# One transformer-like block on one core: another opening for the first four tiles, and the last output tile in column halves

## The chip, the core and the metric

The kernel runs on one core of one Trainium2 chip. A core has five engines that each work through their own list of instructions in order: TensorE (PE in the profile; its weight loads are listed apart as PEld), VectorE (DVE), ScalarE (ACT), GpSimd (POOL) and SyncE (SP), which here only starts transfers. Transfers between the chip's main memory and the core's working memory run on 16 DMA engines. PE writes its results into a small accumulator memory (PSUM), from which ACT or DVE copies them out; a function on ACT needs the right table, which a table load brings in.

The metric is the device time of one execution in microseconds (us), lower is better. Before the change its median over five runs is 233.13 us (232.92 to 233.24).

## The reference

The input is `A_x`, 2048 rows of 512. Every row is normalized to mean 0 and variance 1 (with 1e-5 added to the variance). From the normalized rows `xn` come two branches, and the result puts them together:

```python
xn = _layernorm(x, axis=-1)
s = _A_ref(xn, A_wqkv, A_wo)
g = _silu(_B_ref(xn, B_w_gate, B_w_up, B_w_down))
return x + s * g
```

Branch A is attention with 32 heads of 16: `q`, `k` and `v` are one product with `wqkv` (512 x 1536); each position attends to 8 earlier positions, 2 apart; the heads' outputs go through `wo` (512 x 512). Branch B is a gated network: `gelu(xn @ w_gate) * (xn @ w_up)`, 1792 wide, then `w_down` back to 512. All data are bf16.

## The kernel before

The 2048 rows are 16 tiles of 128 rows. Four tiles make a quarter `j` (`TQ` = 512 rows, `NJ` = 4). A quarter passes through three stages: `qkv` (12 groups of 4 matmuls, one group for each 128 columns of `wqkv`; groups 0 to 3 are q, 4 to 7 k, 8 to 11 v), `glu` (14 steps `fc`, each with a gate group, an up group, their copies on ACT and a product on DVE) and `down` (one step for each of the four tiles: 14 matmuls for y, Silu on ACT, 4 matmuls for s, a product and a sum on DVE, and the store). The attention's own steps (products `pk` and `pv` on DVE, short matmuls on PE) are hung between these by a table of side steps, `at(...)`. The order is written out by hand: `tc.manual_schedule()` keeps the instructions of each engine in the order of the program, and only the waits between engines are added.

Matmuls contract over 128 at a time, so `project` (L219) runs four matmuls over the contraction blocks `dk` into one PSUM tile. Their right operand is `xnT`, the normalized rows transposed. For a tile of rows the way there is:

- `moments` (L169): `bn_stats` and `bn_aggr` on DVE give mean and variance `mv`; DVE adds EPS; POOL raises the sum to the power -0.5, which gives `rstd`.
- `normalize` (L179): one DVE instruction makes `xn`.
- `transpose` (L186): four PE transposes into one PSUM tile `tr`, then one ACT copy into `xnT`. (Quarters 2 and 3 are transposed by DMA.)

PSUM tiles with the tag `mm` share 5 buffers that are taken in turn: `tr`, the q, k and v groups, the gate and up groups, y and s, and the tile that the warm-up writes.

The opening (L452 to L473) is the part of the program that the change rewrites. PE starts with `warm_up(9, TQ)`: nine matmuls of 512 columns on zeros whose result nobody reads. Then come moments of tiles 0 and 1, their normalization and transposes, with two small warm-up matmuls of 128 columns (`warm_up(2, P)`) behind each set of transposes; then moments and normalization of tiles 2 and 3; then moments of tiles 4 to 7 and constants on POOL. The q and k groups of quarter 0 run in two halves of 256 rows: with `hh` = 0 they need tiles 0 and 1 only, and the transposes of tiles 2 and 3 are put in front of groups 3 and 5. The v groups follow with 512 rows at a time.

All loads are started by SP in the order of L93 to L101: x tiles 0 to 3 one by one, then the q, the k and the v third of `wqkv`, then x tiles 4 to 7, and then the gate and up weights with the rest of x.

The end is `down` for tile 15 (L368). There y is one PSUM tile of 512 columns and Silu one ACT instruction of 512, while s, the product, the sum and the store are done in two pieces of 256 columns. The first piece's store is started by SP, the second's by ACT.

Of the kernel before, what the change touches and what calls it, by code (L numbers as in the profile page):

```python
# [9 lines left out]
AF = mybir.ActivationFunctionType  # L10
# [18 lines left out]
def kernel(  # L29
# [81 lines left out]
            )  # L111


    warm = const.tile([P, TQ], BF16, name="warm")
    nc.vector.memset(warm[:], 0.0)
    ident = const.tile([P, P], BF16, name="ident")
    make_identity(nc, ident[:])
# [48 lines left out]
    rstd = const.tile([P, NT, 1], F32, name="rstd")  # L166


    def moments(t):  # L169
        nc.vector.bn_stats(out=stats[:, t, :], in_=x_sb[:, t, :])  # L170
        nc.vector.bn_aggr(out=mv[:, t, :], in_=stats[:, t, :])
        nc.vector.tensor_scalar(  # L172
            out=rstd[:, t, :], in0=mv[:, t, 1:2], scalar1=EPS, scalar2=None, op0=ALU.add
        )
        nc.gpsimd.tensor_tensor(out=rstd[:, t, :], in0=rstd[:, t, :], in1=mhalf[:], op=ALU.pow)  # L175
# [7 lines left out]
            op0=ALU.subtract, op1=ALU.mult,  # L183
        )

    def transpose(t):  # L186
        xn = xns[t]
        tr = mm.tile([P, NC * P], BF16, name="tr", tag="mm")
        for c in range(NC):
            nc.tensor.transpose(tr[:, c * P : (c + 1) * P], xn[:, c * P : (c + 1) * P], ident[:])  # L190
        j, i = divmod(t, TPQ)
        if i == 0:
            xnT[j] = xtp.tile([P, NC, TQ], BF16, name="xnT")
        nc.scalar.activation(  # L194
            out=xnT[j][:, :, i * P : (i + 1) * P],
            in_=tr[:].rearrange("p (c n) -> p c n", c=NC),
            func=AF.Copy,
        )

    def warm_up(n, cols):  # L200

# [14 lines left out]
                transpose=True,  # L216
            )

    def project(ps, w, lo, j, i0=0, n=TQ):  # L219
        for dk in range(NC):  # L220
            nc.tensor.matmul(  # L221
                ps[:],
                lhsT=w[:, dk, lo : lo + P],
                rhs=xnT[j][:, dk, i0 : i0 + n],
                start=(dk == 0),
                stop=(dk == NC - 1),
            )

    st = [dict(pk={}, pv={}) for _ in range(NJ)]

    def qkv(j, fo, i0=0, n=TQ):
        which, c = divmod(fo, NC)
        if fo == 0 and i0 == 0:
            st[j]["q"] = qp.tile([P, NC, TQ], BF16, name="q_sb")
        ps = mm.tile([P, n], F32, name="qkv_ps", tag="mm")
        project(ps, wqkv_sb, fo * P, j, i0, n)
        if which == 0:
            nc.scalar.activation(out=st[j]["q"][:, c, i0 : i0 + n], in_=ps[:], func=AF.Copy)  # L238
        elif which == 1:
            lo = PAD + j * TQ + i0  # L240
            nc.scalar.activation(out=k_sb[:, c, lo : lo + n], in_=ps[:], func=AF.Copy)  # L241
        else:
            vst = sm4.tile([P, TQ], BF16, name="vst")
            nc.scalar.activation(out=vst[:], in_=ps[:], func=AF.Copy)  # L244
            lo = PAD + j * TQ
            nc.sync.dma_start(out=vT[c * P : (c + 1) * P, lo : lo + TQ], in_=vst[:])
# [119 lines left out]
        st[j][fc] = h  # L366

    def down(j, tt):  # L368
        y = mm.tile([P, D], F32, name="y_ps", tag="mm")
        for fc in range(NF):  # L370
            nc.tensor.matmul(  # L371
                y[:],
                lhsT=st[j][fc][:, tt * P : (tt + 1) * P],
                rhs=wd_sb[:, fc, :],
                start=(fc == 0),
                stop=(fc == NF - 1),
            )
        sl = sm2.tile([P, D], BF16, name="sl")
        nc.scalar.activation(out=sl[:], in_=y[:], func=AF.Silu)  # L379
        t = j * TPQ + tt  # L380
        o_t = sm4.tile([P, D], BF16, name="o_t")
        pieces = 2 if t == NT - 1 else 1
        n = D // pieces
        for i in range(pieces):
            cols = slice(i * n, (i + 1) * n)
            s = mm.tile([P, n], F32, name="s_ps", tag="mm")
            for g in range(NC):
                nc.tensor.matmul(  # L388
                    s[:],
                    lhsT=st[j]["oT"][:, g, tt * P : (tt + 1) * P],  # L390
                    rhs=wo_sb[:, g, cols],
                    start=(g == 0),
                    stop=(g == NC - 1),
                )
            m = sm2.tile([P, n], BF16, name="m")
            nc.vector.tensor_tensor(out=m[:], in0=s[:], in1=sl[:, cols], op=ALU.mult)  # L396
            nc.vector.tensor_tensor(out=o_t[:, cols], in0=m[:], in1=x_sb[:, t, cols], op=ALU.add)  # L397
            (nc.scalar if i else nc.sync).dma_start(
                out=out2d[t * P : (t + 1) * P, cols], in_=o_t[:, cols]
            )  # L400


    side = {}
# [46 lines left out]


    HT = TPQ // 2  # L452
    warm_up(9, TQ)
    moments(0)
    moments(1)
    normalize(0)
    transpose(0)
    normalize(1)
    warm_up(2, P)
    transpose(1)  # L460
    warm_up(2, P)
    moments(2)
    moments(3)
    normalize(2)
    normalize(3)
    for t in range(TPQ, 2 * TPQ):
        moments(t)
    sum_constants()
    for hh in range(2):
        for fo in range(2 * NC):  # L470
            qkv(0, fo, hh * HT * P, HT * P)
            if hh == 0 and fo in (2, 4):
                transpose(HT + fo // 2 - 1)  # L473
    for i in range(NC):
        run("qkv", 0, i)
        run("qkv", 0, NC + i)
# [42 lines left out]
```

## Time and profile before

| | |
|---|---|
| median of five runs | 233.13 us (232.92 to 233.24) |
| the profiled execution | 233.13 us |
| its span, first to last instruction | 231.4 us |
| PE busy | 225.4 us (97% of the span) |
| PEld busy | 104.0 us (45%) |
| DVE busy | 146.5 us (63%) |
| ACT busy | 131.8 us (57%), 14 table loads among it |
| POOL busy | 23.6 us (10%) |
| data moved | 23.71 MB |

The span is 1.7 us shorter than the time of the same execution; the profiled execution took as long as the median run. In lines of the timeline the first number is the start in us from the start of the span, the second the duration of the whole group on that line, then engine, line of the program, operation, output and inputs, shape, and the count; square brackets give the idle time of the engine just before and what ended it. The matmuls on a line overlap, so twelve matmuls of 272 ns can take 1.47 us together. In the groups by line, the first number after the bar is the busy time in us, the second the mean duration of one instruction in ns.

### The profile page before, as it was taken

The page shows a single profiled execution, that of the slowest core. Times are in us where ns is not written, and L with a number is a line of the kernel's source. Part 1 is how long each engine was busy: PE and PEld are TensorE (multiplying, and loading weights), DVE is VectorE, ACT ScalarE, POOL GpSimd, SP SyncE. Part 2 cuts the span into 40 slices and gives each one's busy share as a digit, 9 for nine tenths or more (in the row PEclk, how much of TensorE's full clock was granted, in tenths as well). Part 3 has the DMA queues.
Part 4 walks back from the last instruction along what each step waited for, and adds up shares of the span by engine and source line. Part 5 has one row for each costly group of instructions (what it writes and reads, how often), then busy time and mean ns, then how long its engine had stood idle before and what let it go on. Part 6 is the DMA issues. An engine that isn't in the chain of part 4 may idle for free.

```text
span 231.4 us, 3491 instructions
## 1 busy us (share of the span) xinstructions
PE 225.4 (97%) x1313; PEld 104.0 (45%) x1313; DVE 146.5 (63%) x232; ACT 131.8 (57%) x214; POOL 23.6 (10%) x64
## 2 busy tenths in 40 slices
PE   7899999999999999999999999999999999999993
PEld 2775444444444444444444444444444444444441
DVE  4593996997795198981677149941449429864132
ACT  2779879755514865756721595656642396576211
POOL 3258924100000000130000000000000000000000
PEclk9999999999999999999999999999999999999999
DMA  5999499921388211100276711100047800000001
GB/s 143 363 374 371 114 192 203 299 87 48 89 184 193 60 23 28 26 0 0 92 168 142 164 24 31 23 6 0 24 138 162 202 29 0 0 0 4 23 23 45
DMA packets 27057, 23.71 MB, mean 102 GB/s; under 512 B 6688, under 2 KB 27040, under 8 KB 27040
## 3 DMA queue, kind: packets, MB, share of 16 engines
q1 hardware_dynamic: 26896, 23.42, 38.6%
q8 instruction: 10, 0.16, 0.3%
q10 hardware_dynamic: 144, 0.07, 0.1%
q14 instruction: 7, 0.06, 0.1%
HBM read 18.22 MB, written 4.21 MB: 97 GB/s over the span
## 4 chain that ended last, share of the span: by engine, by line
PE 95%; DVE 2%; DMA 1%; ACT 1%; issue 0%
PE g_ps L221 21%; PE u_ps L221 21%; PE y_ps L371 21%; PE qkv_ps L221 18%; PE s_ps L388 6%; PE o_ps L336 3%; PE L_ps L276 3%; PE tr L190 1%; DMA x_sb<-in_A_x_dram 1%; DVE stats L170 1%; PE den_ps L296 0%; PE sp_ps L311 0%; DVE m L396 0%; ACT sl L379 0%; ACT xnT L194 0%; DVE o_t L397 0%
## 5 line engine op out<-in xcount | busy, mean ns | idle before, releaser
L221 PE MATMUL g_ps<-xnT,wg_sb 128*128 128x512 bf16 x224 | 57.6, 379 | 0.0
L221 PE MATMUL u_ps<-xnT,wu_sb 128*128 128x512 bf16 x224 | 57.5, 379 | 0.0
L371 PE MATMUL y_ps<-wd_sb,h 128*128 128x512 bf16 x224 | 51.0, 379 | 0.0
L365 DVE TENSOR_TENSOR h<-ge,u 128x512 bf16<-128x512 bf16 x56 | 23.8, 424 | 34.1 <-ACT u L363 33.9
L266 DVE TENSOR_TENSOR pk<-q_sb,k_sb 128x2048 bf16<-128x2048 bf16 x32 | 37.8, 1220 | 11.6 <-ACT k_sb L241 11.6
L221 PE MATMUL qkv_ps<-xnT,wqkv_sb 128*128 128x512 bf16 (+1 forms) x224 | 43.0, 349 | 0.6 <-ACT xnT L194 0.6
L361 ACT ACTIVATE ge<-g_ps 128x512 bf16<-128x512 f32 x56 | 33.6, 601 | 14.4 <-PE g_ps L221 12.9
L363 ACT ACTIVATE u<-u_ps 128x512 bf16<-128x512 f32 x56 | 33.6, 599 | 13.9 <-PE u_ps L221 13.9
L322 DVE TENSOR_TENSOR pv<-E,v_arr 128x2048 bf16<-128x2048 bf16 x32 | 38.6, 1217 | 0.1
L379 ACT ACTIVATE sl<-y_ps 128x512 bf16<-128x512 f32 x16 | 9.6, 598 | 43.9 <-PE y_ps L371 43.9
L221 PEld LDWEIGHTS <-wu_sb 128*128 128x128 bf16 x224 | 21.9, 98 | 26.6 <-issue 0.3
L371 PEld LDWEIGHTS <-h 128*128 128x128 bf16 x224 | 21.9, 98 | 26.4
L221 PEld LDWEIGHTS <-wg_sb 128*128 128x128 bf16 x224 | 20.8, 98 | 26.6 <-issue 4.2
L221 PEld LDWEIGHTS <-wqkv_sb 128*128 128x128 bf16 x224 | 21.6, 98 | 19.9 <-issue 0.8
L396 DVE TENSOR_TENSOR m<-s_ps,sl 128x512 bf16<-128x512 f32 (+1 forms) x17 | 11.2, 657 | 26.6 <-PE s_ps L388 24.1
L175 POOL TENSOR_TENSOR rstd<-rstd,mhalf 128x1 f32<-128x1 f32 x16 | 10.5, 654 | 78.3 <-DVE rstd L172 78.3
L388 PE MATMUL s_ps<-wo_sb,oT 128*128 128x512 bf16 (+1 forms) x68 | 16.4, 366 | 0.0
L170 DVE BATCH_NORM_STATS2 stats<-x_sb 128x6 f32<-128x512 bf16 x16 | 11.0, 687 | 4.0 <-DMA x_sb<-in_A_x_dram 4.0
L238 ACT ACTIVATE q_sb<-qkv_ps 128x512 bf16<-128x512 f32 (+1 forms) x20 | 10.2, 512 | 5.4 <-PE qkv_ps L221 5.1
L244 ACT ACTIVATE vst<-qkv_ps 128x512 bf16<-128x512 f32 x16 | 9.6, 597 | 5.6 <-PE qkv_ps L221 5.6
L241 ACT ACTIVATE k_sb<-qkv_ps 128x512 bf16<-128x512 f32 (+1 forms) x20 | 10.2, 512 | 3.2 <-PE qkv_ps L221 2.9
L348 DVE TENSOR_TENSOR oT<-o_ps,rb 128x1024 bf16<-128x1024 f32 x8 | 9.7, 1219 | 1.4 <-PE o_ps L336 1.4
(42 smaller groups left out, 110.8 us busy)
## 6 DMA issues: line engine op xcount, KB each, us to landing
v_arr<-vT SPq DMA_DIRECT2D x16, 520.0 KB, 5.1
vT<-vst SPq DMA_DIRECT2D x16, 128.0 KB, 2.6
out_dram<-o_t SPq DMA_DIRECT2D x15, 128.0 KB, 2.5
wg_sb<-in_B_w_gate_dram SPq DMA_DIRECT2D x2, 896.0 KB
wu_sb<-in_B_w_up_dram SPq DMA_DIRECT2D x2, 896.0 KB, 13.8
wd_sb<-in_B_w_down_dram SPq DMA_DIRECT2D x1, 1792.0 KB, 17.1
wqkv_sb<-in_A_wqkv_dram SPq DMA_DIRECT2D x3, 512.0 KB, 5.6
x_sb<-in_A_x_dram SPq DMA_DIRECT2D x3, 512.0 KB, 10.3
```

The costliest lines, as they stand in the source:

```text
L170: nc.vector.bn_stats(out=stats[:, t, :], in_=x_sb[:, t, :])
L175: nc.gpsimd.tensor_tensor(out=rstd[:, t, :], in0=rstd[:, t, :], in1=mhalf[:], op=ALU.pow)
L221: nc.tensor.matmul(ps[:], lhsT=w[:, dk, lo : lo + P], rhs=xnT[j][:, dk, i0 : i0 + n], start=(dk == 0), stop=(dk == NC - 1),)
L238: nc.scalar.activation(out=st[j]["q"][:, c, i0 : i0 + n], in_=ps[:], func=AF.Copy)
L266: nc.vector.tensor_tensor(out=pk[:], in0=st[j]["q"][:], in1=k_sb[:, :, off : off + TQ], op=ALU.mult)
L322: nc.vector.tensor_tensor(out=pv[:], in0=st[j]["E"][:, wh, :].unsqueeze(1).to_broadcast([P, 4, TQ]), in1=st[j]["va"][:, 4 * g : 4 * g + 4, ...
L361: nc.scalar.activation(out=ge[:], in_=g_ps[:], func=AF.Gelu_apprx_tanh)
L363: nc.scalar.activation(out=u[:], in_=u_ps[:], func=AF.Copy)
L365: nc.vector.tensor_tensor(out=h[:], in0=ge[:], in1=u[:], op=ALU.mult)
L371: nc.tensor.matmul(y[:], lhsT=st[j][fc][:, tt * P : (tt + 1) * P], rhs=wd_sb[:, fc, :], start=(fc == 0), stop=(fc == NF - 1),)
L388: nc.tensor.matmul(s[:], lhsT=st[j]["oT"][:, g, tt * P : (tt + 1) * P], rhs=wo_sb[:, g, cols], start=(g == 0), stop=(g == NC - 1),)
L396: nc.vector.tensor_tensor(out=m[:], in0=s[:], in1=sl[:, cols], op=ALU.mult)
```

## The change

There are three parts.

1. *rstd of tiles 0 to 3.* Instead of an addition on DVE and a power on POOL, ACT computes `Sqrt(variance + EPS)` into `std`, and DVE takes its reciprocal. The reciprocal stands at the start of `first_normalize`, so behind both tiles' moments. A Sqrt on a constant at the very start makes ACT load the table for Sqrt first. Tiles 4 to 15 keep the power on POOL.
2. *The opening.* The warm-up is 17 matmuls of 256 columns on a tile of zeros half as wide, and four instead of two small ones behind each set of transposes. The ACT copy of tile 1's transposes is cut in two parts of two contraction blocks each. The first four q groups are no longer done one after another: all four run over contraction blocks 0 and 1, and then all four over blocks 2 and 3. The transposes of tiles 2 and 3 are placed behind the four q groups and behind group 4, and their copies are done by DVE. The moments of tiles 4 to 7 are placed behind the k groups of the first half.
3. *The last tile.* For tile 15, y and Silu are also computed in halves of 256 columns: y, Silu, s, product, sum and store of the left half, then the same of the right half. Both stores are started by SP.

```diff
-    warm = const.tile([P, TQ], BF16, name="warm")
+    warm = const.tile([P, TQ // 2], BF16, name="warm")
...
+    epsc = const.tile([P, 1], F32, name="epsc")
+    nc.gpsimd.memset(epsc[:], EPS)
+    std = const.tile([P, TPQ, 1], F32, name="std")
+
+    nc.scalar.activation(out=std[:, 0, :], in_=epsc[:], func=AF.Sqrt, bias=epsc[:], scale=1.0)
+
+    def first_moments(t):
+        nc.vector.bn_stats(out=stats[:, t, :], in_=x_sb[:, t, :])
+        nc.vector.bn_aggr(out=mv[:, t, :], in_=stats[:, t, :])
+        nc.scalar.activation(
+            out=std[:, t, :], in_=mv[:, t, 1:2], func=AF.Sqrt, bias=epsc[:], scale=1.0
+        )
+
+    def first_normalize(t):
+        nc.vector.reciprocal(out=rstd[:, t, :], in_=std[:, t, :])
+        normalize(t)
...
-    def transpose(t):
+    def transpose(t, parts=1, copy=None):
...
-        nc.scalar.activation(
-            out=xnT[j][:, :, i * P : (i + 1) * P],
-            in_=tr[:].rearrange("p (c n) -> p c n", c=NC),
-            func=AF.Copy,
-        )
+        dst = xnT[j][:, :, i * P : (i + 1) * P]
+        src = tr[:].rearrange("p (c n) -> p c n", c=NC)
+        for k in range(parts):
+            c = slice(k * NC // parts, (k + 1) * NC // parts)
+            if copy is None:
+                nc.scalar.activation(out=dst[:, c], in_=src[:, c], func=AF.Copy)
+            else:
+                copy(out=dst[:, c], in_=src[:, c])
...
-    def project(ps, w, lo, j, i0=0, n=TQ):
-        for dk in range(NC):
+    def project(ps, w, lo, j, i0=0, n=TQ, dks=range(NC)):
+        for dk in dks:
...
-    def qkv(j, fo, i0=0, n=TQ):
+    def qkv(j, fo, i0=0, n=TQ, ps=None):
...
-        ps = mm.tile([P, n], F32, name="qkv_ps", tag="mm")
-        project(ps, wqkv_sb, fo * P, j, i0, n)
+        if ps is None:
+            ps = mm.tile([P, n], F32, name="qkv_ps", tag="mm")
+            project(ps, wqkv_sb, fo * P, j, i0, n)
...
     def down(j, tt):
-        y = mm.tile([P, D], F32, name="y_ps", tag="mm")
-        for fc in range(NF):
-            nc.tensor.matmul(
...
-        nc.scalar.activation(out=sl[:], in_=y[:], func=AF.Silu)
-        t = j * TPQ + tt
+        t = j * TPQ + tt
+        halves = [slice(0, D // 2), slice(D // 2, D)] if t == NT - 1 else [slice(0, D)]
+        n = D // len(halves)
...
+        for i, cols in enumerate(halves):
+            y = mm.tile([P, n], F32, name="y_ps", tag="mm")
+            for fc in range(NF):
+                nc.tensor.matmul(
+                    y[:],
+                    lhsT=st[j][fc][:, tt * P : (tt + 1) * P],
+                    rhs=wd_sb[:, fc, cols],
+                    start=(fc == 0),
+                    stop=(fc == NF - 1),
+                )
+            nc.scalar.activation(out=sl[:, cols], in_=y[:], func=AF.Silu)
             s = mm.tile([P, n], F32, name="s_ps", tag="mm")
...
-            (nc.scalar if i else nc.sync).dma_start(
-                out=out2d[t * P : (t + 1) * P, cols], in_=o_t[:, cols]
-            )
+            nc.sync.dma_start(out=out2d[t * P : (t + 1) * P, cols], in_=o_t[:, cols])
...
     HT = TPQ // 2
-    warm_up(9, TQ)
-    moments(0)
-    moments(1)
-    normalize(0)
-    transpose(0)
-    normalize(1)
-    warm_up(2, P)
-    transpose(1)
-    warm_up(2, P)
-    moments(2)
-    moments(3)
-    normalize(2)
-    normalize(3)
+    HQ = HT * P
+    warm_up(17, TQ // 2)
+    first_moments(0)
+    first_moments(1)
+    first_normalize(0)
+    transpose(0)
+    first_normalize(1)
+    warm_up(4, P)
+    transpose(1, parts=2)
+    warm_up(4, P)
+    first_moments(2)
+    first_moments(3)
+    first_normalize(2)
+    first_normalize(3)
+
+    qs = [mm.tile([P, HQ], F32, name="qkv_ps", tag="mm") for _ in range(NC)]
+    for dks in ((0, 1), (2, 3)):
+        for fo in range(NC):
+            project(qs[fo], wqkv_sb, fo * P, 0, 0, HQ, dks)
+    for fo in range(NC):
+        qkv(0, fo, 0, HQ, qs[fo])
+    transpose(HT, copy=nc.vector.tensor_copy)
+    for fo in range(NC, 2 * NC):
+        qkv(0, fo, 0, HQ)
+        if fo == NC:
+            transpose(HT + 1, copy=nc.vector.tensor_copy)
     for t in range(TPQ, 2 * TPQ):
         moments(t)
     sum_constants()
-    for hh in range(2):
-        for fo in range(2 * NC):
-            qkv(0, fo, hh * HT * P, HT * P)
-            if hh == 0 and fo in (2, 4):
-                transpose(HT + fo // 2 - 1)
+    for fo in range(2 * NC):
+        qkv(0, fo, HQ, HQ)
```

## The prediction

> **What bounds the kernel now.** I read the page's chain first, then the waits of PE, then the timeline of the first 10 us and of the last 5. The chain says PE for 95% of the span, and PE's list of waits has three entries, all before 7.5 us:
>
> ```profile
> PE 95%; DVE 2%; DMA 1%; ACT 1%; issue 0%
> ```
>
> ```profile
> PE warm_ps L204 <- DVE k_sb L161: 1.3, 1, 1.3
> PE qkv_ps L221 <- ACT xnT L194: 0.6, 1, 0.6
> PE tr L190 <- DVE xn L181: 0.2, 1, 0.2
> ```
>
> So PE works without a break from its first q matmul at 7.49 us to its last s matmul, and only two stretches can be shortened: what lies before 7.49, and what follows PE's end. The opening, in order of time:
>
> ```profile
> 1.25 4.02 PE L204 MATMUL warm_ps<-warm 128*128 128x512 bf16 x9 [1.25 <-DVE k_sb L161]
> 3.75 0.18 DVE L171 BATCH_NORM_AGGREGATE mv<-stats 128x2 f32<-128x6 f32 x1
> 4.28 0.55 POOL L175 TENSOR_TENSOR rstd<-rstd,mhalf 128x1 f32<-128x1 f32 x1 [2.86 <-DVE rstd L172]
> 5.05 0.41 DVE L181 TENSOR_SCALAR xn<-x_sb,mv,rstd 128x512 bf16<-128x512 bf16 x1
> 5.51 0.61 PE L190 MATMUL tr<-ident,xn 128*128 128x128 bf16 x4 [0.24 <-DVE xn L181]
> 6.16 1.28 ACT L194 ACTIVATE xnT<-tr 128x512 bf16<-128x512 bf16 x2 [4.08 <-PE tr L190]
> 6.37 0.43 PE L190 MATMUL tr<-ident,xn 128*128 128x128 bf16 x4
> 7.24 0.10 PEld L221 LDWEIGHTS <-wqkv_sb 128*128 128x128 bf16 x1 [0.50 <-DMA wqkv_sb<-in_A_wqkv_dram]
> 7.49 1.47 PE L221 MATMUL qkv_ps<-xnT,wqkv_sb 128*128 128x256 bf16 x12 [0.57 <-ACT xnT L194]
> 9.02 1.04 PE L221 MATMUL qkv_ps<-xnT,wqkv_sb 128*128 128x256 bf16 x8
> 9.28 0.59 ACT L194 ACTIVATE xnT<-tr 128x512 bf16<-128x512 bf16 x1
> ```
>
> The second copy into xnT ends at 6.16 + 1.28 = 7.44 and releases the q matmuls at 7.49. But the weights for them were there only at 7.24: the weight load of that time waited for their DMA. So at most 7.49 - 7.24 = 0.25 us can be had here, however early xnT is. The end of the kernel:
>
> ```profile
> 226.50 1.04 PE L388 MATMUL s_ps<-wo_sb,oT 128*128 128x256 bf16 x8
> 226.69 0.60 ACT L379 ACTIVATE sl<-y_ps 128x512 bf16<-128x512 f32 x1 [3.29 <-PE y_ps L371]
> 227.33 0.42 DVE L396 TENSOR_TENSOR m<-s_ps,sl 128x256 bf16<-128x256 f32 x1 [2.43 <-ACT sl L379]
> 228.00 0.42 DVE L396 TENSOR_TENSOR m<-s_ps,sl 128x256 bf16<-128x256 f32 x1
> 228.45 0.29 DVE L397 TENSOR_TENSOR o_t<-m,x_sb 128x256 bf16<-128x256 bf16 x1
> 228.77 0.38 ACTq L398 DMA_DIRECT2D out_dram<-o_t  x1
> ```
>
> PE ends at 227.54. The first m waited for Silu (227.29); the second had to stand behind the first pair on DVE and started at 228.00, 0.46 after the last s.
>
> **rstd.** The first copy waits for xn of tile 0, and that does not wait for POOL: pow ends at 4.28 + 0.55 = 4.83, xn starts at 5.05, because DVE first finishes the moments of tile 1 and its addition (4.98). Without the two additions, stats of tile 1 can start about 0.10 after the aggregate at 3.75, so at 3.85 instead of 4.04, and its aggregate ends at 4.75. The Sqrt on ACT: two ACT copies of 512 and 256 columns take 0.597 and 0.385, so 0.83 ns a column and 0.17 fixed; one column is at least 0.17 and at most 0.385. I take 0.26, so std of tile 0 is ready at 3.98 + 0.26 = 4.24, hidden by the moments of tile 1 (0.4 us of cover). The reciprocal of 128x1 is bounded by the additions of that shape (0.15) and the reciprocal of 128x128 (0.952); the shape decides, 0.15. So reciprocal 4.67 to 4.82, xn of tile 0 4.86 to 5.27 (0.19 earlier), and xn of tile 1, whose pow held it at 5.90, at about 5.37 to 5.78.
>
> The dummy Sqrt and its constant (one POOL memset of 0.10, done near 1.5) lie in ACT's idle time before 6.16; the table load at 0.80 (1.28 us) was there already and changes only its table. The rule that speaks against this part is that of the Trainium skill, "ScalarE: Activation LUTs", section "Table sets: the hidden batching unit": keep functions of one set together, a switch costs about 2.66 us. The same section says that cheap functions such as copy are in every set. By its rule alone, Sqrt and Copy in turn would cost two more switches, an estimate of 5.3 us from that page's figure. The trace has 14 loads, none before a Copy that follows Gelu, Exp or Silu, so I count none.
>
> **Warm-up and transposes.** The memset is half as long (0.27 now; PE starts at 1.14 instead of 1.25). Nine matmuls of 512 take (4.02 - 0.63) / 8 = 0.424 each; 17 of half the size at 0.213 end at 4.77, where now it is 5.07. Transposes of tile 0 start at 5.32; they are still at the slow rate (0.107 each: the four at 5.51 take 0.61, those at 6.37 only 0.43). Four small warm-up matmuls behind them keep PE until 6.17, past xn of tile 1 (5.78), so these and no longer POOL set the second transposes: 6.17 against 6.37. The fast rate came near 6.5, so the last is done at about 6.72 (now 6.80). This part of the earlier xn is lost.
>
> **Split copy and interleaved q.** Part one of the copy, 256 columns, 0.385: 6.76 to 7.14; part two to 7.43. Matmuls on blocks 0 and 1 could start at 7.19, the weights at 7.24 decide. That the waits go by the piece and not by the whole xnT is seen above: the fourth q group (9.02) ran beside the copy of tile 2 (9.28) that stands ahead of it in the program. Eight matmuls at (1.47 - 0.27) / 11 = 0.109 take until 8.11, well past part two; the fourth PSUM buffer, freed by part two, is asked for at 7.89. So the opening gains 0.25 at most, 0.15 if the first weight load (0.10) has to be over; nothing if a wait on part two is put ahead. I take 0.23.
>
> **What is moved behind it.** Copies of tiles 2 and 3 go to DVE: between 0.41 (xn, same shape) and 0.69 (m, same shape, from PSUM), at 9.41 and 10.12, done by 10.81 at the worst; the second-half q groups want them at about 11.15. If that cover were gone, each 0.1 late would cost 0.1. ACT is relieved of 2 x 0.59, and its Sqrts of tiles 2 and 3 (near 7.4 to 7.8) are over before the first q copy at 8.5. In the interleaved order that copy comes 0.4 later than now (8.12), four copies follow at 0.34 each, and PSUM buffers come free at 8.9, 9.2, 9.6 and 9.9, ahead of PE's need at 9.20, 9.64, 9.86 and 10.30. Here 0.3 is the least cover. The k third of wqkv lands near 8.7 (issued 3.13, median 5.6 to landing); wanted at 9.2. Moments of tiles 4 to 7 wait for their x until 11.71 now, so DVE loses nothing by their new place; POOL's queue loses four pows, and sum_constants stays behind the later ones. SP's queue keeps its order up to the end. From 7.49 on PE has no idle time with a releaser, so a q start 0.23 earlier moves everything by 0.23, unless a transfer is late then: the v products start at 43.6, and their last DMA (issued at 29.8, at most 11.3 to landing) is there by 41.1; if that cover of 2.5 were gone, the gain of the opening would be lost there.
>
> **The last tile.** PE does the same sums in 28 + 8 matmuls of 256 columns: 28 x 0.109 = 3.05 against 14 x 0.216 = 3.02, so 0.03 longer. The extra weight loads (98 ns) fit under 109. The right y is now done 0.44 before PE's end, Silu of 256 columns (0.385, as the copies) ends 0.02 after it, so PE's last s releases the second m. Behind PE alone m starts 0.10 after (223.74 against 223.64 one tile earlier): 227.54 + 0.03 + 0.10 = 227.67 against 228.00. Gain 0.33; bounds 0.25 (Silu as late as 0.1 more) and 0.40. The store moves from ACT's queue to SP's, where nothing is ahead of it but the left store, over 1 us before; same size, same landing, 0.
>
> **Sum** against the profiled 233.13 (which is the median): -0.23 - 0.33 = -0.56, so 232.57 us.
>
> **Rivals.** (1) *The opening gives nothing* (the split copy released late, or weights landing later in other runs): for it, the margin between part one (7.19) and weights (7.24) is only 0.05, and the gain is capped by a DMA; against it, the piecewise waits. Time 233.13 - 0.33 = 232.80: within 0.2%, which is 0.47 us and about what a measurement can tell from no change. The same result if only the opening holds: 232.90.
>
> (2) *The fast rate of PE comes later* and the change is slower. Now PE runs slow from 1.25 to about 6.5, with an idle stretch of some 0.4 between 5.07 and 5.51. The warm-up will end 0.3 earlier and the gap be 0.55. If the rate counted anew from 5.32 and took the same 5.2 us, q work would run at half rate from 7.24 to 10.5 and lose 1.6: 234.2. It decides the sign from a rate change at 7.24 + 2 x 0.56 = 8.4, and makes it slower by 0.2% from 9.3. Against it: between 3.1 and 6.5 PE is busy for 2.75 us now and by my times for 2.87 after, for the eight small matmuls fill up. The Trainium skill, "TensorE: Matmul & The Clock Gate", Part 1, says that a free-running window of about 3.4 us has to be busy; an estimate from that page, one window missed after 6.5, is 1.3 us of loss.
>
> (3) *Copy is not in Sqrt's table*: reloads of 1.28 before the copies and before Sqrt of tiles 2 and 3 put ACT back by some 2.6 at the first q copy, and PE would wait about 1.7 for buffers: 234.3. Only the 14 loads seen speak against it.
>
> **How the numbers follow.** Forecast with both gains at 0.47 or more: 0.50, range 232.35 to 232.66. One gain only, or both with a small stall: 0.32, between 232.66 and 233.6. Slower: 0.18, of which rival 2 0.10, rival 3 0.03, an unseen stall in the new order 0.05. Low end: opening 0.25, tail 0.40, runs 0.2 below the median: 232.3. The high end must take in a first part of the slower cases: 233.5.
>
> **What would show it.** Right: first q matmul at 7.24 to 7.35, 14 table loads, no wait of PE after it, transposes of tile 1 near 6.2, second m within 0.15 of PE's end. Wrong: q matmuls spaced 0.21, a table load between Sqrt and Copy, a PE wait for ACT or DVE between 9 and 11.5, or a last store no earlier after PE's end than the 1.23 us of now.

## The result and the profile after

The changed kernel takes 232.57 us in the median of 21 runs (232.29 to 232.97), against 233.05 us for the kernel before (41 runs). The ratio is 0.9971, with a 95% interval from 0.9959 to 0.9984, so the gain is small but clear of noise: 0.48 us or 0.2% between the medians, and 0.3% by the ratio, which is that of the means and takes in five runs of the kernel before between 234.58 and 235.19 us (the last section says what such runs are). The median stands at the predicted 232.57 us. The forecast change was -0.56 us from 233.13, the measured one is -0.48 us from 233.05; that the two times agree to 0.01 us is luck. The terms of the sum were not all right, as the experiments show.

The first profiled execution of the changed kernel is an unlucky one: it took 233.48 us, more than each of the 21 runs, and its span is 231.8 us where that of before was 231.4. Its list of what PE waited for (us in total, times, longest) says where that comes from:

```profile
PE qkv_ps L241 <- DMA wqkv_sb<-in_A_wqkv_dram: 1.2, 1, 1.2
PE warm_ps L224 <- DVE k_sb L161: 1.1, 1, 1.1
PE tr L207 <- DVE xn L198: 0.3, 1, 0.3
PE o_ps L357 <- DVE pv L343: 0.3, 1, 0.3
```

Two entries are new. The q matmuls wait for their weights and no longer for xnT, and PE waits for a pv product of DVE in the middle of the kernel. The opening of the same execution, from the timeline:

```profile
1.12 3.81 PE L224 MATMUL warm_ps<-warm 128*128 128x256 bf16 x17 [1.12 <-DVE k_sb L161]
4.75 0.41 DVE L198 TENSOR_SCALAR xn<-x_sb,mv,rstd 128x512 bf16<-128x512 bf16 x1
5.22 0.61 PE L207 MATMUL tr<-ident,xn 128*128 128x128 bf16 x4 [0.30 <-DVE xn L198]
5.87 1.33 ACT L216 ACTIVATE xnT<-tr 128x512 bf16<-128x512 bf16 x3 [0.87 <-PE tr L207]
6.05 0.45 PE L207 MATMUL tr<-ident,xn 128*128 128x128 bf16 x4
7.96 1.92 PE L241 MATMUL qkv_ps<-xnT,wqkv_sb 128*128 128x256 bf16 x16 [1.24 <-DMA wqkv_sb<-in_A_wqkv_dram]
```

Everything up to xnT came as forecast or a little earlier: the transposes of tile 0 at 5.22 (5.32 forecast), those of tile 1 at 6.05 (6.17), and the third copy on ACT done at 5.87 + 1.33 = 7.20. But the weights were there only at 7.92. Of the 16 shares into which that transfer is cut, 15 had landed by 6.70 us; one came 1.2 us later. The end of the kernel:

```profile
227.71 0.60 PE L408 MATMUL s_ps<-wo_sb,oT 128*128 128x256 bf16 x4
227.91 0.38 ACT L405 ACTIVATE sl<-y_ps 128x256 bf16<-128x256 f32 x1 [1.58 <-PE y_ps L398]
228.42 0.42 DVE L416 TENSOR_TENSOR m<-s_ps,sl 128x256 bf16<-128x256 f32 x1 [1.21 <-PE s_ps L408]
228.88 0.29 DVE L417 TENSOR_TENSOR o_t<-m,x_sb 128x256 bf16<-128x256 bf16 x1
```

PE ends at 228.31 and the last m starts 0.11 us later, released by PE (before: 0.46 us after PE's end, behind the first pair on DVE). Silu ended at 228.29. The chain that ends last is PE for 92% of the span:

```profile
PE 92%; DVE 3%; DMA 2%; SPq 1%; ACT 0%; issue 0%; DVEq 0%
```

Set against the profile before, this execution splits in three: the first q matmul is 0.47 us later (7.96 against 7.49), the way from there to PE's end is 0.31 us longer (220.35 against 220.04), and what follows PE's end is 0.38 us shorter (3.47 against 3.85); 0.40 us in sum, which is the difference of the spans. So it can't be read as the changed kernel as such; a second profile and the parts one by one were needed.

### The profile page after: what moved, and what is told of

It is laid out like the page before. It is cut to its first block, busy times and chain, and to the rows that moved or that the text cites. A ratio compares the mean times of both kernels' runs of the same rounds, so it can differ in the third digit from the quotient of the medians.

```text
span 231.8 us, 3545 instructions
## 1 busy us (share of the span) xinstructions
PE 225.4 (97%) x1339; PEld 106.9 (46%) x1339; DVE 147.1 (63%) x234; ACT 132.3 (57%) x219; POOL 22.1 (10%) x61
## 4 chain that ended last, share of the span: by engine, by line
PE 92%; DVE 3%; DMA 2%; SPq 1%; ACT 0%; issue 0%; DVEq 0%
PE g_ps L241 21%; PE y_ps L398 21%; PE u_ps L241 20%; PE qkv_ps L241 17%; PE s_ps L408 6%; PE L_ps L297 3%; PE o_ps L357 3%; DMA wqkv_sb<-in_A_wqkv_dram 2%; DVE pv L343 2%; SPq L83 1%; PE tr L207 1%; DVE h L386 0%; PE sp_ps L332 0%; PE den_ps L317 0%; ACT ge L382 0%
## 5 line engine op out<-in xcount | busy, mean ns | idle before, releaser
L398 PE MATMUL y_ps<-wd_sb,h 128*128 128x512 bf16 (+1 forms) x238 | 51.2, 366 | 0.0
L398 PEld LDWEIGHTS <-h 128*128 128x128 bf16 x238 | 23.3, 98 | 25.3
L405 ACT ACTIVATE sl<-y_ps 128x512 bf16<-128x512 f32 (+1 forms) x17 | 9.7, 572 | 44.0 <-PE y_ps L398 44.0
L192 POOL TENSOR_TENSOR rstd<-rstd,mhalf 128x1 f32<-128x1 f32 x12 | 8.0, 666 | 80.5 <-DVE rstd L189 78.3
L408 PEld LDWEIGHTS <-oT 128*128 128x128 bf16 x68 | 6.7, 98 | 7.2
```

Source lines behind the costliest of these rows:

```text
L398: nc.tensor.matmul(y[:], lhsT=st[j][fc][:, tt * P : (tt + 1) * P], rhs=wd_sb[:, fc, cols], start=(fc == 0), stop=(fc == NF - 1),)
L408: nc.tensor.matmul(s[:], lhsT=st[j]["oT"][:, g, tt * P : (tt + 1) * P], rhs=wo_sb[:, g, cols], start=(g == 0), stop=(g == NC - 1),)
```

## The experiments

The times of the kernel before that stand beside each run were taken together with it on the same chip.

**The changed kernel once more.**

> The changed kernel once more, beside the others. If the landing of the q weights at 7.92 us in its first profile was one late transfer of that execution (one DMA engine, the other 15 were done at 6.70), this profile has them near 7.2 us, the first q matmul near 7.25 us and a span some 0.7 us shorter. If the new order delays them, they land near 7.9 us again.

232.58 us (ratio 0.9972, 0.9953 to 0.9990), the same as at first. This profile's span is 230.6 us, with the first q matmul 1.1 us earlier than in the first one:

```profile
6.87 1.92 PE L241 MATMUL qkv_ps<-xnT,wqkv_sb 128*128 128x256 bf16 x16 [0.48 <-ACT xnT L216]
```

The weights landed at 6.82 us. (The line names xnT, but the first part of its copy, which is all that these matmuls need, was done at 6.58; the weights came last.) The late share was one of that execution and not of the new order: no other profile with the old order of loads has the q weights later than 7.39 us. Against before: -0.62 us up to the first q matmul, +0.28 from there to PE's end, -0.39 behind it; -0.73 in sum.

**The last tile alone.** The kernel before, with the new `down`:

```diff
-        y = mm.tile([P, D], F32, name="y_ps", tag="mm")
...
+        for i, cols in enumerate(halves):
+            y = mm.tile([P, n], F32, name="y_ps", tag="mm")
```

> The kernel before with the last tile in column halves and nothing else. My theory: the second product m is released by PE's last s matmul, about 0.10 us after it, instead of standing 0.46 us behind it on DVE; the store comes 0.33 us earlier and the time falls by 0.33 us (ratio 0.9986), with the q start where it is in the kernel before. Rival, that the opening alone brought the gain: 0 to 0.05 us, the last store still 1.2 us after PE's end.

232.71 us against 233.11 (ratio 0.9977, 0.9957 to 0.9997): -0.40 us. From PE's end to the end of the span it takes 3.46 us in the profile, as in the changed kernel, against 3.85, and the last m is released by PE, 0.11 us after its end:

```profile
229.14 0.42 DVE L395 TENSOR_TENSOR m<-s_ps,sl 128x256 bf16<-128x256 f32 x1 [1.22 <-PE s_ps L387]
```

The rival that gave the whole gain to the opening falls. (Its profiled execution took 234.19 us for another reason; see the last section.)

**The opening alone.** The changed kernel with the old `down`.

> The changed kernel with the last tile as before: rstd by Sqrt, the new warm-up, the split copy and the interleaved q groups, nothing at the end. My theory: xnT is ready near 7.0 us and the first q matmul starts as soon as the weights have landed, so the gain is 0.25 us when they land by 7.2 us and turns into nothing when they land after 7.45 us; over several runs 0.1 to 0.25 us. Rival, that the earlier xnT brings its whole lead whatever the weights do: 0.4 to 0.5 us. Rival, that the changed profile's loss before the first q matmul (start at 7.96) belongs to the new order and not to that one execution: 0.4 us slower than before.

233.03 us against 233.11 (ratio 0.9997, 0.9981 to 1.0013): no measurable gain, and less than the 0.1 to 0.25 us of my theory. Yet the first q matmul is at 7.33 us in its profile, 0.16 earlier than before, released by weights that landed at 7.28:

```profile
7.33 1.92 PE L241 MATMUL qkv_ps<-xnT,wqkv_sb 128*128 128x256 bf16 x16 [0.25 <-DMA wqkv_sb<-in_A_wqkv_dram]
```

In the profile the gain is given back later: from the first q matmul to PE's end it takes 220.29 us, 0.25 more than before, and the wait for pv is there again. Both rivals, the one with a gain of 0.4 to 0.5 us and the one with a loss of 0.4 us, fall.

**The wait for pv.** Every profile with rstd by Sqrt shows it, up to here. These lines follow it back in the second profile of the changed kernel, from PE to DVE to POOL (lines of DVE, POOL and PE, put in order of time):

```profile
41.42 0.15 DVE L189 TENSOR_SCALAR rstd<-mv 128x1 f32<-128x1 f32 x1
42.06 0.55 POOL L192 TENSOR_TENSOR rstd<-rstd,mhalf 128x1 f32<-128x1 f32 x1 [2.17 <-DVE h L386]
42.65 0.41 DVE L198 TENSOR_SCALAR xn<-x_sb,mv,rstd 128x512 bf16<-128x512 bf16 x1 [0.73 <-POOL rstd L192]
48.66 0.40 PE L357 MATMUL o_ps<-pv,hsum 128*32 128x512 bf16 x4 [0.26 <-DVE pv L343]
```

And in the kernel before:

```profile
42.03 0.15 DVE L172 TENSOR_SCALAR rstd<-mv 128x1 f32<-128x1 f32 x1
42.34 0.60 POOL L175 TENSOR_TENSOR rstd<-rstd,mhalf 128x1 f32<-128x1 f32 x1 [1.84 <-DVE rstd L172]
42.97 0.41 DVE L181 TENSOR_SCALAR xn<-x_sb,mv,rstd 128x512 bf16<-128x512 bf16 x1 [0.45 <-POOL rstd L175]
48.19 1.23 PE L336 MATMUL o_ps<-pv,hsum 128*32 128x512 bf16 x16
```

It is tile 11, whose rstd is untouched by the change. Before, POOL's pow starts 0.15 us after DVE's addition ends (42.34 - 42.19); after, 0.48 us (42.06 - 41.58). DVE waits 0.28 us longer for it, its products run back to back from there to the one that PE waits for, and PE loses 0.26 us. POOL has three instructions fewer up to this point (four pows less, one memset more). So three were put back:

```diff
         nc.gpsimd.memset(dsum[:], 0.0)
+        for _ in range(3):
+            nc.gpsimd.memset(pad[:], 0.0)
```

> The changed kernel with three small memsets added on POOL behind the moments of tiles 4 to 7, so that POOL's later instructions stand at the same count as in the kernel before. Every profile with the new opening shows POOL's pow for tile 11 starting 0.45 us after its wait instruction, those with the old one 0.11 us, and PE waits 0.26 us longer for pv near 49 us. Theory, that the pause hangs on the place in POOL's list of instructions (three fewer than before): the pause is 0.11 us again, the extra wait of PE is gone and the kernel is 0.26 us faster than the changed one. Rival, that it comes from the times at which DVE and POOL meet in the new opening: the pause stays at 0.45 us and the time is that of the changed kernel within 0.05 us.

In the profile the pause is gone, and the last o_ps follow without a wait:

```profile
41.68 0.15 DVE L192 TENSOR_SCALAR rstd<-mv 128x1 f32<-128x1 f32 x1
41.98 0.59 POOL L195 TENSOR_TENSOR rstd<-rstd,mhalf 128x1 f32<-128x1 f32 x1 [1.84 <-DVE rstd L192]
42.61 0.41 DVE L201 TENSOR_SCALAR xn<-x_sb,mv,rstd 128x512 bf16<-128x512 bf16 x1 [0.44 <-POOL rstd L195]
47.84 1.23 PE L360 MATMUL o_ps<-pv,hsum 128*32 128x512 bf16 x16
```

From the first q matmul to PE's end it takes 220.09 us, 0.23 less than without the memsets. The median is 232.49 us (12 runs; ratio 0.9972, 0.9944 to 0.9999), which by itself can't be told from the changed kernel's 232.57; the 0.26 us that I expected in the time did not show, only 0.23 us on PE's way in the profile. Four further kernels with the three memsets have a pause of 0.09 us between POOL's wait instruction and the pow, the seven profiles with rstd by Sqrt and without them 0.43 to 0.45 us. Counted from the first q matmul, the instructions of DVE and ACT ahead of that pow start within 0.02 us of each other in the kernel before, the changed kernel and this one. So the place in POOL's list of instructions is shown as the cause of the pause; what POOL does in the 0.34 us is not. One candidate is the fetching of instructions, which the profile shows as DMA packets of a kind of their own. No such packet moves during the pause in any of the seven profiles. But the next one starts 0.7 to 1.2 us after the start of the pow in the seven profiles without the pause, and 3.5 to 4.0 us after it in the seven with it. So how the list is cut into fetched pieces changes with the same three instructions, and whether that makes the pause stays open.

**The opening without the pause.** The new opening with the three memsets, and the old `down`:

> The new opening alone with the three memsets on POOL, the last tile as before. It measures the opening's gain without the pause on POOL. If the pause cost the whole opening 0.25 us of its gain (the new opening alone gave 0.08 us), this is 0.25 to 0.4 us faster than the kernel before, near 232.75 us, and from the first q matmul to PE's end it takes 220.04 us as before. If the opening brings nothing by itself, the time is 233.0 us.

232.88 us against 233.12 (ratio 0.9984, 0.9967 to 1.0002): -0.24 us, three times the -0.08 of the opening with the pause, though the interval still takes in no change at all. The first q matmul is at 7.11 us, 0.38 earlier than before:

```profile
7.11 1.91 PE L244 MATMUL qkv_ps<-xnT,wqkv_sb 128*128 128x256 bf16 x16 [0.25 <-ACT xnT L219]
```

The way from there to PE's end is 220.04 us, exactly that of before.

**rstd alone.** The kernel before with `first_moments` and `first_normalize`, its warm-up, whole copies and q groups kept:

```diff
     warm_up(9, TQ)
-    moments(0)
-    moments(1)
-    normalize(0)
+    first_moments(0)
+    first_moments(1)
+    first_normalize(0)
```

> The kernel before with rstd of tiles 0 to 3 by Sqrt and reciprocal, and the old warm-up, copies, order of q groups and last tile. My theory, that the earlier xn is what brings the opening's gain and the split and the interleaving bring little: first q matmul at 6.9 to 7.3 us, time within 0.15 us of the new opening alone. Rival, that the split copy and the interleaving are needed: first q matmul no earlier than 7.4 us and no gain over the kernel before. By the theory on POOL's list its pow for tile 11 pauses 0.45 us here too, and 0.26 us of the gain is lost to pv.

232.98 us against 233.06 (ratio 0.9995, 0.9970 to 1.0021), within 0.05 us of the new opening alone. The first q matmul is at 7.25 us and waits for the weights (landed at 7.21), not for xnT (7.11); the pause of POOL is there. So in that execution Sqrt and reciprocal bring by themselves what the weights leave to be had; in time, with the pause, neither kernel's gain is clear of noise.

**Whole copy, q groups one after another.** The changed kernel without its split copy and without the interleaving:

```diff
-    transpose(1, parts=2)
+    transpose(1)
...
-    qs = [mm.tile([P, HQ], F32, name="qkv_ps", tag="mm") for _ in range(NC)]
-    for dks in ((0, 1), (2, 3)):
-        for fo in range(NC):
-            project(qs[fo], wqkv_sb, fo * P, 0, 0, HQ, dks)
     for fo in range(NC):
-        qkv(0, fo, 0, HQ, qs[fo])
+        qkv(0, fo, 0, HQ)
```

> The changed kernel with the copy of tile 1 in one piece and the first four q groups one after another. If the weights decide, the whole copy (0.60 us, from about 6.54) is ready at 7.14 and still ahead of them: the time is that of the changed kernel within 0.05 us when the weights land at 7.2 us. If the split and the interleaving are what brings the opening's gain, it is 0.2 us slower than the changed kernel.

232.76 us, 0.18 more than the changed kernel that was measured beside it (ratios 0.9983, 0.9968 to 0.9999, and 0.9972, 0.9953 to 0.9990; the intervals overlap). In its profile the weights had landed at 6.79, and this time xnT decided:

```profile
6.76 0.60 ACT L216 ACTIVATE xnT<-tr 128x512 bf16<-128x512 bf16 x1 [0.26 <-PE tr L207]
```

It ended at 7.36, and the q matmuls began at 7.41. In such an execution the split is worth some 0.2 us (an estimate: its first part would have been done at 6.76 + 0.38 = 7.14); in one where the weights come at 7.36 or later, nothing. This execution took 233.17 us, 0.41 more than the median, and PE waits once more in it, 0.28 us for ACT at 135.4 us, so it does not stand for all runs. My expectation that the weights always decide was too simple, and with these runs the size of the split's share is not settled.

**The q weights earlier.**

```diff
-    for t in range(TPQ):
-        load_x(t)
-    for i in range(3):
+    load_x(0)
+    load_x(1)
+    load_w(wqkv_sb, A_wqkv, 0, D)
+    load_x(2)
+    load_x(3)
+    for i in range(1, 3):
```

> The changed kernel with the load of the q weights started ahead of x tiles 2 and 3 instead of behind them. In six profiles the q weights landed between 6.79 and 7.92 us. Theory, that they cap the opening in part of the executions: they land by 6.3 us, the first q matmul starts 0.05 us after the first part of the copy of tile 1 (6.6 to 7.15 us), and the time falls by 0.1 to 0.4 us against the changed kernel, with a narrower spread. Rival, that xnT alone sets the start: no difference beyond 0.05 us. If the later x tiles 2 and 3 hurt, PE waits for their transposes near 9 us.

232.79 us against 233.06 (ratio 0.9982, 0.9962 to 1.0002), and a wider spread, 232.27 to 233.56. The weights landed at 6.15, and xnT (6.89) released the first q matmul at 6.94, as expected; but there is no gain over the changed kernel. Tiles 2 and 3 of x come later (6.50 and 6.86 instead of 3.9 and 4.4 in the second profile of the changed kernel), and the k weights are the next to be waited for: they land at 9.01, and the first k group starts at 9.05. PE has no idle time there yet. In the combined kernel below, which has the same order of loads, it has:

```profile
9.89 0.61 PE L247 MATMUL qkv_ps<-xnT,wqkv_sb 128*128 128x256 bf16 x4 [0.67 <-DMA wqkv_sb<-in_A_wqkv_dram]
```

There one share of the k weights landed at 9.84, 15 of them by 8.17. So the cap can move from one transfer to the next, which I did not expect. A share of the k weights as late as that came once with the old order too (9.94, in the kernel with four pieces below), so that the new order makes it more frequent is not shown. As a remedy this falls.

**Three pieces at the end.** The combined kernel has the earlier q weights, the three memsets, and the last tile in 256, 128 and 128 columns:

```diff
-        halves = [slice(0, D // 2), slice(D // 2, D)] if t == NT - 1 else [slice(0, D)]
-        n = D // len(halves)
+        cuts = [0, D // 2, 3 * D // 4, D] if t == NT - 1 else [0, D]
+        halves = [slice(lo, hi) for lo, hi in zip(cuts, cuts[1:])]
...
+            n = cols.stop - cols.start
```

> The changed kernel with the q weights loaded ahead of x tiles 2 and 3, three memsets on POOL, and the last tile cut into 256, 128 and 128 columns. If the three causes add up: 0.26 us from POOL, 0.1 to 0.4 us from the weights, and 0.2 us at the end, where the last product and sum handle 128 columns (about 0.31 and 0.22 us by the step from 512 to 256 columns, against 0.42 and 0.29 us); together 0.5 to 0.9 us below the changed kernel, near 232.0 us. If POOL's pause stays, 0.3 us more.

232.32 us (231.92 to 233.56; ratio 0.9969, 0.9950 to 0.9987), 0.3 us more than forecast: the earlier q weights add nothing, as above. From PE's end to the end of the span it takes 3.10 us, 0.37 less than with halves. With the loads in their old order:

> The changed kernel with the three memsets on POOL and the last tile in 256, 128 and 128 columns, the loads in the changed kernel's order. If the two gains add up: 0.23 us from pv and 0.37 us at the end against the changed kernel (the end after PE's last matmul was 3.10 us with these pieces and 3.47 with halves), so near 232.0 us; if the earlier load of the q weights had its part in the combined kernel's best executions, 232.2 us or more.

231.94 us against 232.99 (5 runs, 231.87 to 232.12; ratio 0.9957, 0.9944 to 0.9970). This is the fastest kernel here, 0.43% under the one before. It lies 1.05 us under the kernel before where the changed one lies 0.48 and 0.53 under it, so 0.5 to 0.6 us under the changed one; the two terms (0.23 and 0.37) add up to 0.60. Five runs are few, and the ranges of its neighbours reach further up. Its last pieces:

```profile
226.66 0.39 PE L412 MATMUL s_ps<-wo_sb,oT 128*128 128x128 bf16 x4
227.17 0.29 DVE L420 TENSOR_TENSOR m<-s_ps,sl 128x128 bf16<-128x128 f32 x1 [0.46 <-ACT sl L409]
227.50 0.22 DVE L421 TENSOR_TENSOR o_t<-m,x_sb 128x128 bf16<-128x128 bf16 x1
```

The last sum is done 0.67 us after PE's end (227.05), against 0.86 with halves, and the last store lands 2.14 us after it, against 2.41 to 2.43.

With the last 128 columns cut in two once more, four pieces in all:

> As with 256, 128 and 128 columns, but the last 128 cut into 64 and 64. Product and sum of 128 columns took 0.29 and 0.22 us against 0.42 and 0.29 for 256, so 64 columns would take 0.23 and 0.19; Silu 0.22 against 0.28. That is 0.15 us less after PE's end. Theory, that only the chain behind PE counts: 0.1 to 0.15 us faster than with thirds. Rival, that matmuls of 64 columns run no faster than those of 128 (0.056 us each, their weights still have 128 columns) and PE ends 0.4 us later: 18 matmuls more at 0.04 to 0.056 us, so 0.3 to 0.9 us slower.

232.42 us (231.67 to 233.55; ratio 0.9973, 0.9960 to 0.9986): no gain over three pieces, and a wide spread. The profile shows neither of the two causes that I had written down. Matmuls of 64 columns are faster than those of 128 (0.029 us apart, not 0.056), and PE needs only 0.05 us more for the last tile, so the rival falls; and the last sum is done 0.63 us after PE's end, 0.04 earlier than with three pieces. But SP starts the last store only 1.30 us after PE's end (with three pieces: 0.70), because starting the store before took it 1.08 us and not 0.33. The line has the four starts together:

```profile
227.02 2.86 SPq L422 DMA_DIRECT2D out_dram<-o_t  x4
```

That execution also had one late share of the k weights (9.94), for which PE waited 1.0 us. During the long start, from 228.13 to 229.01, a packet of fetched instructions moves that no other kernel here has near its end. With one profile, whether that is the cause, and whether the long start is a rule, stays open.

**A short warm-up.** The changed kernel with `warm_up(4, TQ // 2)` in place of 17:

> The changed kernel with 4 instead of 17 warm-up matmuls at the start; the small ones stay. PE is then busy from 1.1 to 2.0 us and idle until the transposes at 5.2 us. By rival 2 of the prediction (the fast rate needs a stretch of some 3.4 us in which PE was mostly busy) the full rate comes between 8.4 and 13.7 us, the q matmuls are spaced 0.213 us until then, and the time is 0.7 to 3.4 us above the changed kernel. If the rate followed the first matmuls alone, or came anyway some 5 us after the start, the time is the changed kernel's.

234.40 us against 232.99 (ratio 1.0056, 1.0043 to 1.0069), 1.8 us above the changed kernel. The first 16 q matmuls take 2.79 us instead of 1.92, and the transposes of tile 1, at 5.92, still 0.63:

```profile
5.92 0.63 PE L207 MATMUL tr<-ident,xn 128*128 128x128 bf16 x4
7.43 2.79 PE L241 MATMUL qkv_ps<-xnT,wqkv_sb 128*128 128x256 bf16 x16 [0.45 <-ACT std L178]
```

(The weights, landed at 7.39, came last before these matmuls, not std.) The full rate came at 9.26 us. So the warm-up earns its place, and rival 2 of the prediction names a real mechanism. Nothing of it shows in the changed kernel itself: neither of its two profiles has a loss of the rate, and the highest of its 32 timed runs (21 and 11) is 233.22 us.

## Why the prediction was right, and where it was not

**The last tile** was sized well. Forecast -0.33 us: measured -0.40 for the part alone, and in the profiles 0.38 to 0.39 less behind PE's end with 0.04 more on PE. Silu of the right half did finish just ahead of PE, m was released by PE 0.11 us after its end (0.10 forecast), and the store on SP's queue cost nothing.

**The opening's gain before the first q matmul** was capped by a number that is no bound. I read 7.24, the moment of the weight load in one profile, as one. Over the profiles that keep the order of loads, the q weights land between 6.75 and 7.92 us, and the first q matmul follows the later of weights and xnT:

| kernel | full rate of PE from | q weights landed | xnT ready | first q matmul |
|---|---|---|---|---|
| before | 6.48 | 7.20 | 7.44 | 7.49 |
| new last tile alone (old opening) | 3.92 | 6.84 | 7.25 | 7.30 |
| changed, first profile | 6.17 | 7.92 | 6.92 | 7.96 |
| changed, second profile | 5.00 | 6.82 | 6.58 | 6.87 |
| new opening alone | 6.90 | 7.28 | 7.12 | 7.33 |
| rstd alone | 6.94 | 7.21 | 7.11 | 7.25 |
| with three memsets, halves | 5.26 | 7.08 | 6.49 | 7.13 |
| with three memsets, three pieces | 5.85 | 6.88 | 6.77 | 6.92 |
| with three memsets, four pieces | 4.18 | 6.75 | 6.44 | 6.80 |
| opening with three memsets | 6.46 | 7.04 | 7.06 | 7.11 |

(xnT ready is the end of the copy, or of its first part, that the first q matmul needs; all in us.) The median of the first q matmul over the seven profiles with the whole new opening is 7.11 us. That is 0.38 us before the 7.49 of the kernel before, but only 0.19 before the 7.30 of the other profile with the old opening, in which the full rate came early. In time the opening without the pause gave 0.24 us, with an interval that takes in no gain. So the 0.23 us that I took is not refuted as a size; its reason, a fixed moment at which the weights land, is. The steps up to xnT were right to about 0.1 us where the full rate came at the same time: Sqrt of 128x1 took 0.295 us (0.26 taken), the reciprocal 0.15 (0.15), the DVE copy 0.42 (0.41 to 0.69). On Sqrt, the Trainium skill, "ScalarE: Activation LUTs", section "What ACT_TABLE_LOAD costs", gives about 280 ns for the fixed cost of an ACTIVATE with a pointer as bias, which the 295 ns measured here bear out to some 5%. There are 14 table loads in the changed kernel as before, and none between Sqrt and Copy, so rival 3 falls. The two further switches, which the rule of the same page's section "Table sets: the hidden batching unit" would give if it is taken alone, did not come; that agrees with the section's other statement, that copy is in every set. (The 2.66 us for a switch, which the prediction puts into that section, stand in the page's section "What ACT_TABLE_LOAD costs". The trace of before has half of that: 1.31 us from the end of one ACTIVATE to the start of the next with a load between them, 186.33 to 187.64.)

**The step that failed** is "POOL's queue loses four pows", counted at nothing. POOL is busy for only 22 of 232 us, but with three instructions fewer its pow for tile 11 starts after a pause that is 0.34 us longer, and behind it DVE runs without slack up to a wait of PE: +0.25 us in the profile of the opening alone, and in time -0.08 us for the opening where it gave -0.24 with the three memsets. The sign that the prediction sets for being right, no wait of PE after the first q matmul, failed with it, and so did a first q matmul at 7.24 to 7.35 (7.96 and 6.87 in the two profiles); 14 table loads, the transposes of tile 1 near 6.2 (6.05 in the first profile) and the last m within 0.15 us of PE's end came.

That the sum came out at the measured median is luck. In times, each with an interval of 0.3 us or more to either side: the tail gave -0.40 where -0.33 was forecast, the opening -0.08 where -0.23 was, and the kernel before measured 0.08 us less than the 233.13 that the sum starts from.

**The rivals.** Rival 1, that the opening gives nothing, came nearest to the truth by its number for the opening alone, but not by its mechanism. The split copy is not released late: the first q matmul starts before the second part is done (7.33 against 7.39 with the new opening alone, 6.92 against 7.04 with three pieces). And weights that land later than 7.4 us came in one of the twelve profiles with the old order of loads. Its 232.80 us is 0.23 more than measured: 0.08 by its base, 0.07 by the tail and 0.08 by the opening. Rival 2 did not come true in any profile of the new opening with the long warm-up. The 2.75 and 2.87 us by which the prediction argues against it seem to count the matmuls from start to start; by the profile's own count PE was busy for 3.14 us of the 3.41 before the full rate in the kernel before, and for 3.11 in the first profile of the changed one.

## What to carry to other kernels

A point in one profile at which a transfer landed is a draw, not a bound: look at several executions before a term is capped by it, and expect that behind an earlier transfer the next one may be what is waited for. Where a chain without slack passes through a nearly idle engine, removing instructions from that engine isn't free by itself; compare its pauses instruction by instruction after the change. At the end of a kernel, cut the last piece of work so that the chain behind the bounding engine's last instruction handles as little as possible: 512 to 256 columns gave 0.38 us behind PE's end, and 256 to 128 another 0.37; 64 columns gave 0.04 us more up to the last sum and nothing in the time.

## What the runs showed of the hardware

**PE's full rate comes and goes in steps of 3.41 us.** The profiled execution of the kernel with only the new last tile had the full rate at 3.92 us, lost it at 7.34 and had it again at 10.75. Its stretches (busy time in us and number of instructions of PE, PEld, DVE, ACT and POOL, then the granted clock, the share of the DMA engines and GB/s):

```profile
1.30:3.92 2.62, 2.62 (x7) 0.95 (x8) 0.98 (x4) 0.78 (x1) 0.12 (x2) 1.00 0.75 195
3.92:7.34 3.42, 1.81 (x17) 0.93 (x16) 2.84 (x10) 1.19 (x2) 1.30 (x3) 1.00 0.95 282
7.40:10.70 3.30, 3.30 (x19) 2.43 (x19) 1.43 (x5) 1.38 (x4) 1.04 (x2) 0.50 1.10 353
```

PE was busy for 1.81 of the 3.42 us before the loss. (The clock column starts too high: up to 3.9 us the warm-up matmuls ran at half rate, 0.43 us apart.) This is what makes 234.19 us of that execution, with the old opening: the way from the first q matmul to PE's end takes 1.70 us more than before. In the kernel with four pieces at the end, the full rate came at a similar time, 4.18 us, and stayed; there the new opening kept PE busy for 2.38 of the next 3.41 us:

```profile
4.18:7.59 3.41, 2.38 (x28) 1.76 (x27) 3.20 (x13) 1.95 (x6) 0.00 (x0) 1.00 0.95 306
```

Less was enough in the first profile of the changed kernel, in which PE waited for the late weights. It was busy for 2.17 of 3.41 us, and the rate stayed:

```profile
6.17:9.58 3.41, 2.17 (x24) 1.84 (x23) 2.12 (x8) 1.70 (x7) 0.00 (x0) 1.00 1.03 343
```

So the limit for keeping the rate lies here between 53% (1.81 of 3.42) and 64% (2.17 of 3.41) busy. The Trainium skill, "TensorE: Matmul & The Clock Gate", Part 1, describes a free-running window of 3413 ns that has to be busy; the steps of 3.41 us agree, and the first full rate at anything from 3.92 to 7.06 us after the kernel's start, with the long warm-up, agrees with "free-running". If steps of that length are laid back from the first full rate, gaining it took more than keeping it. The step that brought it in the kernel with only the new last tile was busy for 2.67 us (78%; first line). In the kernel with the whole copy, a step with 2.53 us (74%; second line) did not bring it, and the next did (third line):

```profile
0.51:3.92 3.41, 2.67 (x7) 1.00 (x8) 1.29 (x6) 1.28 (x1) 0.55 (x3) 1.00 0.58 150
0.24:3.65 3.41, 2.53 (x12) 1.79 (x13) 0.85 (x3) 1.58 (x2) 0.78 (x8) 1.00 0.51 124
3.65:7.06 3.41, 3.07 (x22) 2.33 (x21) 3.23 (x11) 1.49 (x4) 0.00 (x0) 1.00 0.94 285
```

Part 4 of the same page says that transposes do not count as busy in the same way. These steps speak against leaving them out: without the eight transposes the third line has 2.45 us (72%), less than the second, and yet it brought the rate. For keeping it, the two shares without transposes would be 39% and 61%.

The record of each run has its mean granted clock, the share of the full rate that PE was allowed, and it tells what single long executions are. The profiled one that lost a step has 0.993. The 16 runs with 0.992 or 0.993 took 1.48 to 2.43 us more than the median of their kernel; every other run with the clock on record has at least 0.996 and lies at most 1.25 us above it. With the old warm-up and order these are 14 of 127 runs, with the new opening and the long warm-up 2 of 120 (234.3 and 234.4 us with halves and three memsets). So the new opening loses the rate more rarely, though not never, which medians do not show; which of its parts does it, no run here tells.

**One share in 16 of a load can come more than a microsecond late.** Seen for the q weights (15 shares by 6.70, the last at 7.92) and twice for the k weights (8.17 and 9.84; 8.18 and 9.94). The loads behind it then have a late share too: in the first of these executions the last shares of the k weights, the v weights and x tiles 4 to 7 landed at 9.42, 10.92 and 12.42, each 0.77 to 0.78 us behind the other 15. Where PE waits for the weights this goes into the time (1.2, 0.7 and 1.0 us of idle time in the three executions).

**The place of an instruction in POOL's list can cost 0.34 us**, as told above: 0.43 to 0.45 us from a wait instruction to its pow at one place, 0.09 three instructions further on. It cost PE about 0.25 us, because the products on DVE behind that pow have no slack.
